# TensorE's order in the head of an attention-and-MLP kernel: short dummies, out products close behind kv, casts on other engines

## The chip, the core and the metric

The kernel runs on one core of one Trainium2 chip. The metric is the device time of one execution in microseconds (us). Executions of one kernel agree within some 0.3%, so every comparison below is of several runs made on the same chip, and a difference counts as faster or slower only from 2% up. Smaller differences are read from the intervals and from the traces.

Engines in the profile: PE is TensorE's matmuls, PEld its weight loads, DVE is VectorE, ACT is ScalarE, POOL is GpSimd, SP is SyncE, which issues most transfers. PEclk is the TensorE clock that the throttle granted, 1.00 being full.

## The reference

Linear attention over 8 batches of 8 heads, 576 tokens of 64 features, and then an MLP with a Swish of learned slope over all 4608 tokens.

```python
def _attn_ref(q, k, v):
    q_s = exp(q - max over features);  q_s = q_s / sum over features
    k_s = exp(k - max over tokens);    k_s = k_s / sum over tokens
    kv = np.einsum('bhsd,bhse->bhde', k_s, v)
    return np.einsum('bhsd,bhde->bhse', q_s, kv)

def _moe_ref(x, w_in, w_out, beta):      # x: 4608 x 512, w_in: 512 x 2048
    h = x @ w_in
    g = h * (1.0 / (1.0 + np.exp(-beta * h)))
    return g @ w_out                     # 4608 x 512, float32
```

## The kernel before

All matmuls are bf16. Each batch's attention is done while the MLP of an earlier batch keeps TensorE busy. Only batch 0 has nothing to hide behind: its attention is the *head*, about 16 us from the start to the unbroken stream of MLP matmuls. Heads are taken in pairs, 0 to 3 (the prediction says "head 1" for pair 1, and "third kv group" for that of pair 2). For each pair TensorE makes a group of 18 small matmuls (*kv*), VectorE takes the reciprocal of the key sums and writes the scaled product to KVD, four transposes (*turns*) bring the queries to QT, and one matmul of 512 columns (*out product*) makes XT from KVD and QT. Tiles: EQ and GT hold exponentials (GT holds those of the keys here), VF and VB values in fp32 and bf16, WST staged weights, WIN and WOUT weights in bf16. Most matmuls come from one helper, so their line is L373 whatever they do; they are told apart by their tiles.

Dummies keep TensorE busy while it waits for data; `long` makes one in fp32:

```python
def warm(n, bk, long=False):
    for _ in range(n):
        if long:
            mm(PS[bk][:, :], <XT8 as fp32, 128 columns>, <XT8 as fp32, 512 columns>, ...)
        else:
            mm(PS[bk][:, :], WARM[:, 0:128], WARM[:, :], ...)      # bf16, 512 columns
...
def kv_tiles(hp, bk):
    for j in range(NG):                  # 9 token groups, 2 heads: 18 matmuls of 64x64
        for e_ in range(2):
            ...
    ksum_inv(0, bk, hp, 1, D, 1)         # VectorE: reciprocal RC
    kvd(0, hp, bk, 0)                    # VectorE: two scalings, KVD

def out_now(b, hp, bk, eng):
    out_mm(b, hp, bk)                    # KVD x QT, 512 columns
    add(eng, ...)                        # copy to XT
```

The head, in program order:

```python
warm(3, 0, True)
exp_q(0)
...
norm_main(0, 0, 1)                       # normalize queries of pair 0, VectorE
norm_main(0, 1, 1, POOL)
go(t_steps(0, (0,), (3,)))               # turns of pair 0
turn_beta()
warm(1, 0, True)
norm_main(0, 2, 1, POOL)
norm_main(0, 3, 1, POOL)
kv_tiles(0, 7)
go(t_steps(0, (1,), (4,)))
warm(1, 0, True)
cast_v(0, 2)
cast_v(0, 3, POOL, 1)                    # second part of the last values, GpSimd
cast_win(0, 1, POOL)
cast_win(0, 2, POOL)
cast_win(1, 0, POOL)
go(t_steps(0, (2,), (5,)))
kv_tiles(1, 1)
out_now(0, 0, 0, ACTE)
go(t_steps(0, (3,), (6,)))
warm(1, 3)
out_now(0, 1, 5, ACTE)
kv_tiles(2, 7)
cast_v(0, 3, ACTE, 0)                    # first part of the last values, ScalarE
cast_win(0, 0, DVE)
warm(1, 3)
kv_tiles(3, 1)
out_now(0, 2, 0, ACTE)
...
at(0)                                    # first four MLP matmuls
out_now(0, 3, 7, DVE)
at(1)
cast_win(0, 3, DVE)
```

SyncE issues nearly all transfers in program order. `load(3)`, which brings the queries, keys and values of batch 3, stands at the end of block t = 0; the DMA transposes of the queries of batch 2 stand in block t = 1, behind it:

```python
# end of t == 0
tr_dma(0)
load(3)                                  # queries, keys, values (1152 KB), query remainders
...
# t == 1
t_dma(2, 0, 2)                           # transposes of pairs 0, 1 of batch 2
...
t_dma(2, 2, 2)                           # pairs 2, 3
```

The softmax here doesn't subtract the row's maximum and nothing guards it: scores larger than these inputs give would overflow.

## Time and profile before

| | before |
|---|---|
| median, first three runs (284.8 to 285.46) | 285.43 us |
| profiled execution, span | 283.1 us |
| TensorE busy | 98% of the span |
| first MLP matmul of the head | 14.99 us |
| out product of pair 3; MLP without a break from | 15.86; 16.08 us |

A profile line of a timeline reads: start us, busy us, engine, line, operation, output tile <- input tiles, shape, count, and in brackets the idle time ahead of it with what ended it. The prediction below shows the page's shares, the chain and the timelines of the head. In the page, the span is cut into 40 slices of 7 us, and this row gives the granted clock in tenths:

```profile
PEclk9999999999999999999999999999999999999999
```

The view of windows gives, for a stretch of time, its length, each engine's busy us (with instruction count), the granted clock, the share of transfer engines in use and GB/s. The two stretches cover most of the head:

```profile
core 0: us, PE busy (x) PEld busy (x) DVE busy (x) ACT busy (x) POOL busy (x), PEclk, DMA share, GB/s
6.83:10.24 3.41, 3.41 (x38) 2.34 (x37) 2.37 (x8) 2.73 (x5) 2.60 (x3) 1.00 1.03 398
10.24:13.66 3.42, 3.09 (x50) 1.60 (x48) 2.33 (x8) 2.18 (x5) 1.60 (x3) 1.00 0.97 341
```

The clock is full from 6.83 us to the end of the program, and the transfer engines have no time to spare in the head (share about 1).

### The profile page before, as it was taken

The page shows a single profiled execution, that of the slowest core. Times are in us where ns is not written, and L with a number is a line of the kernel's source. Part 1 is how long each engine was busy: PE and PEld are TensorE (multiplying, and loading weights), DVE is VectorE, ACT ScalarE, POOL GpSimd, SP SyncE. Part 2 cuts the span into 40 slices and gives each one's busy share as a digit, 9 for nine tenths or more (in the row PEclk, how much of TensorE's full clock was granted, in tenths as well). Part 3 has the DMA queues.
Part 4 walks back from the last instruction along what each step waited for, and adds up shares of the span by engine and source line. Part 5 has one row for each costly group of instructions (what it writes and reads, how often), then busy time and mean ns, then how long its engine had stood idle before and what let it go on. Part 6 is the DMA issues. An engine that isn't in the chain of part 4 may idle for free.

```text
span 283.1 us, 3950 instructions
## 1 busy us (share of the span) xinstructions
PE 277.9 (98%) x1608; PEld 136.3 (48%) x1608; DVE 117.0 (41%) x218; ACT 177.6 (63%) x243; POOL 38.1 (13%) x57
## 2 busy tenths in 40 slices
PE   7899999999999999999999999999999999999995
PEld 3545454445455445544554445444544444444443
DVE  4665786218781348124831473055705300110012
ACT  6767787989978926795579636892660076017500
POOL 6622041216121032100130000000000000000000
PEclk9999999999999999999999999999999999999999
DMA  7999999999998999217960033002700030012022
GB/s 249 371 390 400 391 371 307 361 341 248 330 329 248 358 360 296 39 34 251 374 104 1 2 148 74 2 1 98 141 4 0 9 141 0 0 54 96 0 74 74
DMA packets 41467, 50.07 MB, mean 177 GB/s; under 512 B 20325, under 2 KB 28773, under 8 KB 40297
## 3 DMA queue, kind: packets, MB, share of 16 engines
q1 hardware_dynamic: 40496, 48.77, 55.1%
q10 hardware_dynamic: 952, 1.06, 1.1%
q8 instruction: 12, 0.20, 0.3%
q14 instruction: 7, 0.05, 0.0%
HBM read 36.71 MB, written 9.44 MB: 163 GB/s over the span
## 4 chain that ended last, share of the span: by engine, by line
PE 98%; DVE 0%; ACT 0%; issue 0%
PE PS L373 97%; PE PS L371 1%; ACT XT L544 0%; DVE XT L219 0%; DVE KVD L411 0%; ACT VB L358 0%; DVE O2S L734 0%; DVE RC L520 0%
## 5 line engine op out<-in xcount | busy, mean ns | idle before, releaser
L655 ACT ACTIVATE GT<-PS,BETA 128x512 bf16<-128x512 f32 x144 | 96.7, 689 | 79.1 <-PE PS L373 79.1
L373 PE MATMUL PS<-WOUT,GT 128*128 128x512 bf16 (+2 forms) x592 | 132.8, 373 | 0.0
L373 PE MATMUL PS<-XT,WIN 128*128 128x512 bf16 x576 | 132.2, 379 | 0.0
L373 PEld LDWEIGHTS PS<-XT,WIN 128*128 128x128 bf16 x576 | 60.2, 106 | 59.2 <-ACT GT L655 0.4
L373 PEld LDWEIGHTS PS<-WOUT,GT 128*128 128x128 bf16 x592 | 55.4, 98 | 61.8
L713 DVE COPY O2S<-PS 128x512 f32<-128x512 f32 x33 | 22.7, 687 | 107.7 <-PE PS L373 107.7
L373 PE MATMUL PS<-VB,EK 128*128 128x65 bf16 x252 | 33.3, 193 | 0.0
L358 POOL CAST VB<-VF 128x576 bf16<-128x576 f32 (+1 forms) x29 | 21.1, 729 | 77.9 <-DMA VF<-in_v_dram 73.5
L309 ACT ACTIVATE EK<-KF 64x1152 bf16<-64x1152 f32 x24 | 27.8, 1157 | 0.4
L339 DVE TENSOR_REDUCE QS<-EQ 128x8 f32<-128x512 bf16 (+1 forms) x22 | 20.1, 913 | 15.4 <-ACT EQ L297 15.3
L373 PEld LDWEIGHTS PS<-VB,EK 128*128 128x128 bf16 x252 | 20.0, 98 | 6.5
L449 DVE CAST XT<-PS 128x512 bf16<-128x512 f32 x24 | 16.4, 690 | 10.9 <-PE PS L373 10.9
L297 ACT ACTIVATE EQ<-QF 128x512 bf16<-128x512 f32 x32 | 17.8, 619 | 2.0 <-DMA QF<-in_q_dram 1.8
L341 DVE TENSOR_TENSOR EQ<-EQ,QI 128x1024 bf16<-128x1024 bf16 (+1 forms) x14 | 15.9, 1132 | 0.5
L373 PE MATMUL PS<-QT,KVD 128*128 128x512 bf16 x32 | 12.2, 380 | 0.3 <-DVE KVD L411 0.3
L341 POOL TENSOR_TENSOR EQ<-EQ,QI 128x512 bf16<-128x512 bf16 x8 | 8.3, 1042 | 17.3 <-DVE QI L340 17.0
L373 PE MATMUL PS<-XT 128*128 128x512 f32 x10 | 7.7, 903 | 1.5 <-DVE XT L219 1.5
L411 DVE TENSOR_TENSOR KVD<-PS,RC 64x64 bf16<-64x64 f32 (+2 forms) x28 | 8.6, 308 | 0.9
L297 ACT ACT_TABLE_LOAD x6 | 7.7, 1283 | 0.1
L655 ACT ACT_TABLE_LOAD x5 | 6.4, 1283 | 0.1
L432 DVE RECIPROCAL RC<-PS 128x4 f32<-128x4 f32 (+2 forms) x9 | 1.6, 177 | 10.0 <-PE PS L373 9.9
L319 ACT ACTIVATE EK<-KF 64x576 bf16<-64x576 f32 (+1 forms) x6 | 5.0, 842 | 1.0 <-DMA KF<-in_k_dram 0.9
(54 smaller groups left out, 85.9 us busy)
## 6 DMA issues: line engine op xcount, KB each, us to landing
out_dram<-O2S SPq DMA_DIRECT2D x8, 1024.0 KB, 5.1
KF<-in_k_dram SPq DMA_DIRECT2D x6, 1152.0 KB, 8.4
VF<-in_v_dram SPq DMA_DIRECT2D x6, 1152.0 KB, 11.2
QF<-in_q_dram SPq DMA_DIRECT2D x6, 1024.0 KB, 7.6
KF<-in_k_dram SPq DMA_DIRECT2D x8, 288.0 KB, 8.3
VF<-in_v_dram SPq DMA_DIRECT2D x8, 288.0 KB, 8.6
WST<-in_moe_w_in_dram SPq DMA_DIRECT2D x8, 256.0 KB, 7.9
O2S<-in_moe_w_in_dram SPq DMA_DIRECT2D x4, 512.0 KB, 11.9
```

Source lines behind the costliest of these rows:

```text
L297: add(ACTE, lambda e, o=o, a=a: e.activation(o, a, ACT.Exp), r=[("qf", i, hp)], w=[("eq", i, hp)])
L309: add(ACTE, lambda e, o=o, a=a: e.activation(o, a, ACT.Exp), r=[("kf", i, h) for h in hps], w=[("ek", i, h, e_) for h in hps])
L319: add(ACTE, lambda e: e.activation(o, a, ACT.Exp), r=[("kf", i, h) for h in hps], w=[("ek", i, h, e_) for h in hps])
L339: add(DVE, lambda e: e.tensor_reduce(s_, a, AX.X, ALU.add), r=ks, w=[("qs", i, hp0)])
L341: add(eng, lambda e: e.tensor_tensor(a, a, vb, ALU.mult), r=ks + [("qi", i, hp0)], w=ks)
L358: add(eng, lambda e: (e.copy if eng == ACTE else e.tensor_copy)(o, a), r=[("vf", i, hp), ("vone", i)], w=[("vb", i, hp, h) for h in ((0, 1 ...
L371: add(PE, lambda e: e.transpose(o, l, r_), r=r, w=w, bank=[bk])
L373: add(PE, lambda e: e.matmul(o, l, r_, start=start, stop=stop, tile_position=tp), r=r, w=w, bank=[bk])
L411: add(DVE, lambda e, o=o, a=a, s_=s_: e.tensor_tensor(o, a, s_, ALU.mult), r=[("ps", bk)] + [("rc", i, h) for h in hps], w=[("kvd", i, h, ...
L449: add(eng, lambda e: (e.copy if eng == ACTE else e.tensor_copy)(XT[i][:, hp, :], PS[bk][:, :]), r=[("ps", bk)], w=[("xt", i, hp)], bank=[bk])
L655: add(ACTE, lambda e: e.activation(GT[:, f, :], PS[bk][:, :], ACT.Silu, scale=BETA[:, f:f + 1]), r=[("ps", bk), "beta"], w=[("gt", f)], ba ...
L713: add(eng, lambda e: (e.copy if eng == ACTE else e.tensor_copy)(O2S[t % 2][:, u, :], PS[bk][:, :]), r=[("ps", bk)], w=[("o2", t % 2, u)], ...
```

## The change

Its intent is to start the MLP matmuls earlier. The first fp32 dummy goes, the second becomes bf16, and one bf16 dummy is added ahead of kv 1; the turns of pair 1 stand ahead of kv 0 instead of behind it; out product 1 moves behind kv 2, and out product 2 *ahead* of kv 3; GpSimd casts the last values whole (before, GpSimd and ScalarE shared them), and casts weight blocks 1 to 3 of the first quarter, so that VectorE casts only block 0.

```diff
@@ -618,29 +618,28 @@
         norm_main(0, 1, 1, POOL)
         go(t_steps(0, (0,), (3,)))
         turn_beta()
-        warm(1, 0, True)
         norm_main(0, 2, 1, POOL)
         norm_main(0, 3, 1, POOL)
+        go(t_steps(0, (1,), (4,)))
         kv_tiles(0, 7)
-        go(t_steps(0, (1,), (4,)))
-        warm(1, 0, True)
+        warm(1, 0)
         cast_v(0, 2)
-        cast_v(0, 3, POOL, 1)
-        cast_win(0, 1, POOL)
-        cast_win(0, 2, POOL)
+        cast_v(0, 3)
+        for m in range(1, NM):
+            cast_win(0, m, POOL)
         cast_win(1, 0, POOL)
         go(t_steps(0, (2,), (5,)))
+        warm(1, 0)
         kv_tiles(1, 1)
         out_now(0, 0, 0, ACTE)
         go(t_steps(0, (3,), (6,)))
         warm(1, 3)
+        kv_tiles(2, 7)
         out_now(0, 1, 5, ACTE)
-        kv_tiles(2, 7)
-        cast_v(0, 3, ACTE, 0)
         cast_win(0, 0, DVE)
         warm(1, 3)
+        out_now(0, 2, 0, ACTE)
         kv_tiles(3, 1)
-        out_now(0, 2, 0, ACTE)
 
         orot = [0]
 
@@ -678,7 +677,6 @@
         at(0)
         out_now(0, 3, 7, DVE)
         at(1)
-        cast_win(0, 3, DVE)
         read_beta()
```

## The prediction

> **What bounds the kernel now.** I first read busy shares, then the chain of work that ended last, then TensorE's own timeline for the head. The page's first line of numbers (engine, busy us, share of the span, instructions) says that TensorE is all but always at work.
>
> ```profile
> PE 277.9 (98%) x1608; PEld 136.3 (48%) x1608; DVE 117.0 (41%) x218; ACT 177.6 (63%) x243; POOL 38.1 (13%) x57
> ```
>
> The chain (start us, us, what) shows where it is not. From 14.99 us it is TensorE work to the very end, so whatever advances the start of the dense matmuls, and is not eaten by a later wait, comes off the time one for one. Between 11.9 and 15 us the chain leaves TensorE twice: for a reciprocal and the two scalings that make KVD, and for a cast of values on ScalarE.
>
> ```profile
> 11.92 0.17 DVE RC L520
> ...
> 12.36 0.24 DVE KVD L411
> 12.60 0.05 issue
> 12.64 0.40 PE PS L373
> 13.05 0.02 issue
> 13.07 0.59 ACT XT L544
> 13.66 0.36 ACT VB L358
> 14.02 0.14 issue
> 14.16 0.80 PE PS L373 x19
> ```
>
> TensorE's timeline (start, us, operation, idle before) shows what the head is made of: two fp32 dummy pairs (8.15, 9.85), four kv groups of 18 small matmuls, and out products with 512 columns.
>
> ```profile
> 8.15 1.12 PE L373 MATMUL PS<-XT 128*128 128x512 f32 x2
> 9.21 0.47 PE L373 MATMUL PS<-VB,GT 64*64 64x65 bf16 x18
> 9.61 0.40 PE L371 MATMUL PS<-IDB,EQ 128*128 128x128 bf16 x4
> 9.85 1.08 PE L373 MATMUL PS<-XT 128*128 128x512 f32 x2
> 10.76 0.39 PE L371 MATMUL PS<-IDB,EQ 128*128 128x128 bf16 x4
> ...
> 14.56 0.39 PE L373 MATMUL PS<-QT,KVD 128*128 128x512 bf16 x1
> 14.99 1.04 PE L373 MATMUL PS<-XT,WIN 128*128 128x512 bf16 x4
> 15.86 0.38 PE L373 MATMUL PS<-QT,KVD 128*128 128x512 bf16 x1
> ```
>
> GpSimd's timeline sets when the third values are there (11.57) and when the last half is; the whole last tile can start at 12.23, when its transfer lands.
>
> ```profile
> 8.61 2.16 POOL L341 TENSOR_TENSOR EQ<-EQ,QI 128x512 bf16<-128x512 bf16 x2 [0.31 <-DVE QI L340]
> 10.90 0.67 POOL L358 CAST VB<-VF 128x576 bf16<-128x576 f32 x1
> 12.23 0.40 POOL L358 CAST VB<-VF 128x256 bf16<-128x256 f32 x1 [0.66 <-DMA VF<-in_v_dram]
> 13.82 1.58 POOL L580 CAST WIN<-WST 128x512 bf16<-128x512 f32 x2 [1.19 <-DMA WST<-in_moe_w_in_dram]
> ```
>
> **What the Trainium skill says.** "FP8 and Floating Point Precision", TensorE Precision Notes: true fp32 takes four passes through the array. The trace agrees: the pair at 9.85 holds TensorE until 10.76, 0.91 us, about four times the 0.22 us step of a bf16 matmul of 512 columns (15.86 to 16.08). "TensorE: Matmul & The Clock Gate", Part 1: the array runs at half rate until it has been busy for a window of about 3.4 us and falls back after an idle one. The trace agrees with the first half: the six opening fp32 passes start 0.85 us apart, the pair at 9.85 about 0.45; no run yet shows the fall back. "SBUF — State Buffer", SBUF: two separate sides: VectorE and GpSimd share one port pair, held exclusively. The trace is consistent: GpSimd's weight cast took 0.83 us where it met VectorE's weight cast and 0.62 us otherwise.
>
> **The change part by part.** The dummies fall from 1.06 and 0.91 us to 0.22 each; four bf16 ones remain. That alone ends nothing: the kv groups and transposes then wait for data. So I laid the new order by hand on the old durations and landings. The steps, read start to start: kv to the next TensorE instruction 0.41; kv to its reciprocal 0.83 (12.96 to 13.79); reciprocal and both KVD scalings 0.68; to TensorE 0.06. So an out product can't follow its kv group by less than 1.57 us. Transposes to a dummy 0.22, to kv 0.32; out to kv 0.32; 512 columns 0.22. A handover from GpSimd to TensorE isn't visible; 0.1 is an estimate between 0.06 (VectorE) and 0.14 (ScalarE, the issue row before 14.16).
>
> - Turns of head 1: their queries are normalized by GpSimd at 8.30, so 8.36. kv 0: 8.68 (before 9.21). Dummy 9.08. Turns 2 wait for GpSimd (9.65): 9.71. Dummy 9.93. kv 1: 10.15 (before 11.08; values ready 9.87). VectorE does the turn copy, reciprocal and scalings of head 0 by 10.42, so out 0 at 10.56 finds its operand there. Turns 3: 10.83 (queries 10.77). Dummy 11.05.
> - kv 2 could go at 11.27 but its values are cast on GpSimd until 11.57: 11.68 (before 12.96, 1.28 us gained). Out 1 right behind it, 12.09: KVD 1 is ready at 11.7. Dummy 12.30.
> - Out 2 now stands ahead of kv 3 and waits for KVD 2: 11.68 + 1.57 = 13.25. So TensorE idles about 0.7 us here; this is a new wait.
> - kv 3: 13.25 + 0.32 = 13.57 (before 14.16, 0.59 gained). Its values, whole on GpSimd, take 12.23 + 0.67 = 12.90 and are off the path; the ScalarE half cast, which ended at 14.01 behind two evictions, is gone.
> - First four weight matmuls at 13.57 + 0.41 = 13.98 (before 14.99, 1.0 gained). Weight block 0 lands at 13.09 and VectorE casts it after KVD 2, 13.22 to 13.65: just in time.
> - Out 3 follows four matmuls, 0.87 us, so at 14.85, but needs KVD 3, 13.57 + 1.57 = 15.13: a second new wait, 0.29 us. Before, this operand was early (14.16 + 1.57 = 15.73 against 15.86). The gain shrinks from 1.0 to 0.73 us: dense work resumes at 15.35 instead of 16.08.
> - Weight blocks 1 to 3 of the first quarter on GpSimd: landings 13.77, 14.45, 15.13, casts of 0.62, last one ready about 16.1; it is needed at 17.1. VectorE loses one 0.43 us cast that wasn't on the path.
>
> Sum: 16.08 - 15.35 = **0.73 us** of 283.1.
>
> **Is it kept?** The weights and the next batch arrive at the transfer engines' pace (share 1.0 or above from 10 to 60 us), and landings don't move. So I checked what TensorE meets between 15 and 49 us after moving 0.73 earlier.
>
> ```profile
> 27.04 1.95 DVE L569 TENSOR_SCALAR WOUT<-WST,RB 128x512 bf16<-128x512 f32 x4 [1.80 <-DMA WST<-in_moe_w_out_dram]
> 39.10 2.08 DVE L569 TENSOR_SCALAR WOUT<-O2S,RB 128x512 bf16<-128x512 f32 x4
> 29.03 9.44 PE L373 MATMUL PS<-WOUT,GT 128*128 128x512 bf16 x43
> 39.84 0.61 PE L371 MATMUL PS<-IDB,EQ 128*128 128x128 bf16 x8
> ```
>
> The first output weights are ready at 27.80 and would be wanted at 28.30 instead of 29.03. The tightest place is at 39 to 40: turns of the next batch wanted at 39.11 plus 0.22 for its last head, normalized by 39.18 before and some 0.2 earlier after (VectorE's preceding work can move up only to the landing at 33.55); output weights 12 wanted at 39.55, ready near 39.4. Both fit by 0.1 to 0.4. At 46 the last values of batch 1 are cast at 45.39 and wanted at 45.9. So I keep the 0.73 whole; a landing 0.3 us late would cost perhaps 0.2 of it.
>
> **The rivals.** (1) The waits eat everything: new idle time of some 0.7 us ahead of out 2 and 0.3 ahead of out 3. For it: the 1.57 us latency is now met twice in a row. Against: kv 2 itself starts 1.28 earlier. If GpSimd's cast of the third values ended 0.5 us later, the gain would be 0.2: 285.2. (2) The clock falls back: from 8.2 to 13.3 TensorE would be idle in gaps totalling about 1.7 us, and a bf16 dummy fills little. Against: no gap reaches a whole window, the longest is 0.7. If it fell for one window, half of 3.4 us is lost (an estimate from the page named): 285.43 - 0.73 + 1.7 = 286.4. (3) The gain is hidden by the transfers' pace at 39 to 46 us: then 0.2 to 0.5 remains: 285.0 to 285.2. (4) The dummies' 1.53 us counted in full: 283.9; against it, each of the four kv groups waits for data that the dummies don't delay.
>
> **Range and chances.** Predicted 285.43 - 0.73 = 284.7 us. The runs before spread over 0.66 us, and rivals 1 and 3 lie within 285.2; rival 4 gives the lower side, a median drawn high the upper: 283.9 to 285.6. Two per cent is 5.7 us, eight times the gain: faster 0.01, same 0.97, slower 0.02.
>
> **What would show it.** In the profile after: kv groups starting near 8.7, 10.15, 11.7 and 13.6; idle time ahead of the third out product (0.6 to 0.8, released by VectorE's KVD) and the fourth (0.2 to 0.4); dense matmuls from about 15.35; no idle TensorE later. Wrong if fp32-like steps (0.4 us per 512 bf16 columns) appear after 8 us, or if TensorE waits for WOUT, EQ or VB after 28 us.

## The result, and the profile after

| | before | after |
|---|---|---|
| median | 285.12 us (4 runs) | 284.88 us (4 runs) |
| all runs | 284.8, 285.43, 285.46, 284.79 | 285.38, 285.06, 284.6, 284.7 |
| mean granted clock of those runs | not on record (profiled execution: 1.0) | 0.994, 0.994, 1.0, 1.0 |
| span of the profiled execution | 283.1 us | 283.6 us |

The ratio is 0.9994, with a 95% interval from 0.9971 to 1.0016: the same. Ratios here and below are the mean time of one kernel's fast runs over that of the other's fast runs of the same rounds, so they are not quite the ratio of the medians quoted beside them. The time is inside the predicted range and 0.2 us from the predicted value.

The row of clocks above already shows something new: two runs of four at 0.994. Of the kernel before, 33 later runs have their clock on record, and all have at least 0.998. The profiled execution (285.38 us) is one of them. The page of the kernel after, its shares and its clock row:

```profile
PE 276.3 (97%) x1575; PEld 136.4 (48%) x1606; DVE 116.4 (41%) x217; ACT 177.2 (62%) x242; POOL 39.3 (14%) x58
...
PEclk9799999999999999999999999999999999999999
```

The second slice has fallen from 9 to 7. The view of windows finds where (columns as before):

```profile
7.29:10.71 3.42, 2.75 (x37) 2.00 (x37) 2.85 (x9) 2.71 (x4) 2.77 (x3) 1.00 1.04 400
10.71:14.12 3.41, 3.08 (x43) 1.87 (x44) 1.92 (x9) 1.94 (x4) 1.59 (x3) 0.50 1.01 347
14.12:17.53 3.41, 3.12 (x29) 1.37 (x30) 1.99 (x7) 2.56 (x4) 2.75 (x4) 1.00 1.05 396
```

For 3.41 us the granted clock is exactly one half, and then full again. Half a rate missing for 3.41 us is as much as a whole one for 1.7 us, 0.6% of the span, which is the 0.994 of the run. TensorE's timeline of the same head shows it instruction by instruction:

```profile
9.22 0.48 PE L373 MATMUL PS<-VB,GT 64*64 64x65 bf16 x18 [0.48 <-ACT VB L358]
...
12.74 0.70 PE L373 MATMUL PS<-VB,GT 64*64 64x65 bf16 x18
13.37 0.61 PE L373 MATMUL PS<-QT,KVD 128*128 128x512 bf16 x1
...
14.44 0.38 PE L373 MATMUL PS<-QT,KVD 128*128 128x512 bf16 x1
14.75 0.47 PE L373 MATMUL PS<-VB,GT 64*64 64x65 bf16 x18
15.15 1.04 PE L373 MATMUL PS<-XT,WIN 128*128 128x512 bf16 x4
16.32 0.39 PE L373 MATMUL PS<-QT,KVD 128*128 128x512 bf16 x1
```

A kv group takes 0.70 us instead of 0.47, an out product 0.61 instead of 0.39. Its first kv group is late for another reason: in this execution the first keys landed at 7.73 us, in the profiled execution of before at 6.58. So this head is *behind* that of before: the last out product is at 16.32 instead of 15.86, and 0.46 us of delay stay to the end. I read this delay from ScalarE's 144 Swish instructions and VectorE's output copies, which are all in the record: each stands 0.46 us later than in before, from 18 us to the last, and 0.46 is also the difference of the unrounded spans. One profile was therefore not enough to say what the change is worth.

The chain of waits of this execution needs care. It leaves TensorE just ahead of the MLP stream for a cast of weights on GpSimd:

```profile
16.11 0.63 POOL WIN L580
16.76 10.74 PE PS L373 x49
```

That is not a real wait. The out product ahead of it is 0.46 us later than before and the Swish instructions after it too, so TensorE lost nothing between. In this trace 16 of the 576 matmuls of this kind have no record, and where one is missing a stretch looks idle.

Two theories of why the head's expected 0.73 us hardly show in the time. **Theory A** (H in the expectations): the clock falls in some executions, because the new head gives the array less work; without falls most of the gain would be there. **Theory B** (T there): the gain of the head is real but is taken back later by a transfer at its own pace. The runs below speak for both.

### The profile page after: what moved, and what is told of

Its sections match the earlier page's. It is cut to its first block, busy times and chain, and to the rows that moved or that the text cites. A ratio compares the mean times of both kernels' runs of the same rounds, so it can differ in the third digit from the quotient of the medians.

```text
span 283.6 us, 3916 instructions
## 1 busy us (share of the span) xinstructions
PE 276.3 (97%) x1575; PEld 136.4 (48%) x1606; DVE 116.4 (41%) x217; ACT 177.2 (62%) x242; POOL 39.3 (14%) x58
## 3 DMA queue, kind: packets, MB, share of 16 engines
q10 hardware_dynamic: 952, 1.06, 1.1%
## 4 chain that ended last, share of the span: by engine, by line
PE 93%; DMA 3%; SPq 2%; issue 1%; POOL 1%; DVE 0%; POOLq 0%
PE PS L373 92%; DMA WST<-in_moe_w_in_dram 3%; SPq L259 1%; POOL WIN L580 1%; SPq L249 0%; PE PS L371 0%; SPq L576 0%; DVE O2S L732 0%; POOLq L140 0%
## 5 line engine op out<-in xcount | busy, mean ns | idle before, releaser
L373 PE MATMUL PS<-XT,WIN 128*128 128x512 bf16 x560 | 130.7, 379 | 0.5
L358 POOL CAST VB<-VF 128x576 bf16<-128x576 f32 x29 | 21.6, 746 | 77.9 <-DMA VF<-in_v_dram 48.8
L373 PE MATMUL PS<-QT,KVD 128*128 128x512 bf16 x29 | 11.2, 387 | 0.2
L373 PE MATMUL PS<-XT 128*128 128x512 f32 x6 | 5.5, 1088 | 1.5 <-DVE XT L219 1.5
L373 PEld LDWEIGHTS PS<-QT,KVD 128*128 128x128 bf16 x32 | 3.1, 98 | 5.6 <-DVE KVD L411 1.2
```

The lines of the kernel that those rows point to most:

```text
L358: add(eng, lambda e: (e.copy if eng == ACTE else e.tensor_copy)(o, a), r=[("vf", i, hp), ("vone", i)], w=[("vb", i, hp, h) for h in ((0, 1 ...
L373: add(PE, lambda e: e.matmul(o, l, r_, start=start, stop=stop, tile_position=tp), r=r, w=w, bank=[bk])
```

## The experiments

Each call had its own chip, with 11 interleaved runs of the kernel before. Medians of before: 285.01, 284.81 and 284.81 us. "Held" and "fell" below say whether a run's mean clock was at least 0.998, or 0.994 (one window of 3.41 us at half rate) and lower. All kernels gave the right result. One measure is an estimate of mine: the *work share* of a 3.41 us window, from durations in these traces, which counts 0.86 us for an fp32 dummy, 0.21 for a bf16 matmul of 512 columns, 0.054 for a turn of 128 columns, 0.24 for a kv group of 18, and of the opening fp32 dummies the part that runs inside the window. (The expectation of c3 below quotes an earlier, rougher count of mine.)

### The changed kernel again (a1_again)

No edit, five rounds.

> The changed kernel as it is, to separate two things that its first profile mixes: the granted clock fell to half from 10.7 to 14.1 us, and the first K tile landed at 7.73 us instead of 6.58. In its first four runs the two with mean clock 0.994 took 285.4 and 285.1, the two with 1.0 took 284.6 and 284.7. Theory H (the clock falls back in some runs and eats the gain): runs at clock 0.994 lie 0.4 to 0.8 us above those at 1.000, and the latter are 0.3 to 0.8 below the kernel before. Rival D (the landing of the first tiles decides, the clock is a passenger): times split by the landing, not by the clock. Rival N (no gain at all, only scatter): both groups have the same time as the kernel before.

Median 284.99 us (284.89 to 285.13), ratio 0.9999 [0.9987, 1.0011]. Two runs of five had fallen (285.10, 284.97), three had held (285.13, 284.99, 284.89). So the falls are a property of the changed kernel, and here they cost nothing: means of 285.04 and 285.00. This is a miss for theory H, which expected 0.4 to 0.8 us between the groups. And a gain of 0.73 us lies outside this interval: 0.0013 of 285 us is 0.37. The profiled execution had fallen, from 8.36 to 11.78 us. Its first keys had landed at 6.93 us, ahead of those of a profiled execution below that held (c2, 7.42), so a late landing of the first keys (rival D) is not needed for a fall. In it the first transposes of batch 2 landed at 71.25 us, 0.5 us before their use at 71.77. Nothing waited here, but a head faster by more than 0.5 us would have.

### More bf16 dummies (a2_fill)

```diff
-        warm(1, 0)
+        warm(2, 0)
...
-        warm(1, 0)
+        warm(2, 0)
...
-        warm(1, 3)
+        warm(2, 3)
...
-        warm(1, 3)
+        warm(4, 3)
```

> The changed kernel with more bf16 dummies in the holes: 2, 2, 2 and 4 in place of 1, 1, 1 and 1 (six more, of 0.216 us each, placed where TensorE waits). Theory H: no run with the clock below 1.0; median 284.6 to 284.8, at most 0.1 above the changed kernel's undisturbed runs. Rival (dummies only delay): 0.2 to 0.6 us slower than the changed kernel at the same clock.

Median 285.25 us (284.55 to 286.08), ratio 1.0013 [0.9996, 1.003]. Two runs of six still fell, at 286.06 and 286.08; those that held have a mean of 285.02. That no run would fall was a miss: ten dummies instead of four did not suffice. The profiled execution had held, with work shares of 39% and 57% in its two windows of the head, and its MLP matmuls began at 14.15. It then lost 0.66 us (by the Swish instructions) where one weight block landed late in this execution: at 18.05 us (before: 15.86), cast on GpSimd from 18.11 to 18.72. So this profile does not say what the dummies cost:

```profile
18.78 10.54 PE L373 MATMUL PS<-XT,WIN 128*128 128x512 bf16 x47 [0.49 <-POOL WIN L580]
```

### Out product 2 behind kv 3 again (a3_kv3first)

```diff
-        out_now(0, 2, 0, ACTE)
         kv_tiles(3, 1)
+        out_now(0, 2, 0, ACTE)
```

> The changed kernel with one part undone: the third out product behind the fourth kv group again, as before. My working says the new order of these two costs time, since the fourth kv group then waits for KVD of the third head: kv 3 could start near 13.0 instead of 13.6 and the out product behind it would find its operand; dense matmuls resume some 0.4 to 0.5 us earlier. Expected 284.1 to 284.4 at clock 1.0. Rival: the dense part meets transfers later (output weights wanted before they land at 27.8 and 39.4), so at most 0.2 us shows. Where the clock falls, 0.5 more.

Median 285.06 us (284.55 to 285.33), ratio 0.9996 [0.9984, 1.0008]. Three runs of five fell (285.06, 285.33, 285.19), two held (284.56, 284.55): 0.64 us between the means. The held runs miss the expected 284.1 to 284.4. The place of out product 2 does not bring the falls about: the four profiled falls (after, a1, a3, a4) begin at 8.36 to 10.71 us, ahead of these two instructions, and this order falls about as often.

### No bf16 dummies in the head (a4_nodummy)

The four `warm` lines are removed from the changed kernel.

> The changed kernel without the four bf16 dummies. Theory H: activity in the head falls further, so the clock falls in more runs than in the changed kernel (more than half), and the median is 285.2 or more. Rival (the small dummies do nothing for the clock): as many fallen runs as in the changed kernel, same times.

Median 286.3 us (284.64 to 286.93), ratio 1.0033 [1.0008, 1.0058]. All six runs fell. Those with one window at half rate (0.994) took 284.89 and 284.64, the one at 0.987 took 286.04, the three at 0.982 (three windows) 286.55 to 286.93. So dummies do act on the clock, and the less array work the head holds, the more windows are lost. This is the dose for which theory A asks. The profiled execution (284.89, one fall) was 0.44 us ahead of before after the head, and lost 0.41 of it in a wait for the DMA transposes at 71.57 us: theory B's place again.

### Values of batch 3 issued later, in both kernels (c1_before_vlate, c2_after_vlate)

```diff
-                load(3)
+                load_main("qf", qt_h, QF, 3)
+                load_k(3)
+                load_qrem(2)
...
                     t_dma(2, 2, 2)
+                    load_v(3)
```

> The kernel before with one transfer moved: the values of batch 3 (1.15 MB) are issued behind the two transposes of batch 2's queries instead of ahead of them. In the profiles so far those transposes landed at 70.5 us in the kernel before and at 71.2 to 71.8 in five others, and the first out product of batch 2 starts at 71.6 in the kernel before. Theory T (the stream of transfers, full from 2 to 70 us, is a second bound at 71.6 us): the transposes land before 70 us; the kernel before mostly gains nothing, since there they were just in time, but its slower runs near 285.5 vanish: 284.7 to 285.0, no run above 285.2. Rival (the landing is never the bound): no change in median or scatter.

> The changed kernel with the same transfer moved. Theory T: a run at clock 1.0 shows the head's whole gain of 0.5 to 0.75 us: 284.1 to 284.5; a run at clock 0.994 lies 0.3 to 1.0 above that. If the gain were eaten in the head alone, runs at clock 1.0 stay at 284.7 to 285.1.

Before with the move: median 284.87 us, ratio 0.9999 [0.9986, 1.0012] from four runs (284.69 to 285.02). Its first run took 754.87 us and is left out as slow. TensorE alone was stretched: it is busy for 737.6 us, at some 0.6 us a matmul of 512 columns (49 in 29.36 us), while ScalarE has its usual 178.4 us. The run is listed at clock 1.0, but its page has no clock row, so that says nothing. I have no cause for it. It was the profiled one, so this kernel has no profile that can be compared.

After with the move: median 284.84 us (284.25 to 285.21), ratio 0.9997 [0.9985, 1.0009]. Three runs held (284.70, 284.42, 284.25) and three fell (284.98, 285.19, 285.21): means of 284.46 and 285.13, so one fall costs 0.67 us where nothing later hides it. The held runs are 0.35 us below the median of before; two of the three lie in the expected 284.1 to 284.5. The transposes landed at 68.90 and 70.62 us, and there is no wait for them. But the profiled execution lost 0.15 of its 0.38 us of head gain earlier, between 46.5 and 47.7 us: the last keys of batch 1 landed late (44.59 us, before: 43.30), ScalarE did their exponentials late, its copy of outputs came behind them, and TensorE's weight load waited for that copy. ScalarE's and TensorE's lines:

```profile
44.61 1.39 ACT L319 ACTIVATE EK<-KF 64x576 bf16<-64x576 f32 x2 [0.44 <-DMA KF<-in_k_dram]
...
47.00 0.33 PEld L373 LDWEIGHTS PS<-XT,WIN 128*128 128x128 bf16 x3 [0.38 <-ACT O2S L711]
```

SyncE's timeline shows what the move did to the issue of batch 2's transposes, for before:

```profile
66.01 3.76 SPq L459 DMA_TRANSPOSE QT<-EQ  x2
```

for the changed kernel with the long dummy (c3_long1, next), whose load order is that of before:

```profile
65.36 4.73 SPq L459 DMA_TRANSPOSE QT<-EQ  x2
```

and for the changed kernel with the move:

```profile
65.78 2.95 SPq L459 DMA_TRANSPOSE QT<-EQ  x2
```

Issued 0.65 us earlier, c3's transposes still landed 0.87 us later than those of before (71.35 against 70.48): the queue ahead of them sets when they land. In the ten profiles with the old load order the first of them landed between 70.48 and 71.78 us, in the three with the values behind them between 68.37 and 69.09. The Trainium skill, "DMA: Bandwidth & Descriptors", section Two DMAs through the same engine are not ordered, says that within one queue of one transfer engine descriptors start in order, though they may overlap. These landings are consistent with that: 1152 KB of values that nobody wants soon stood ahead of transposes that TensorE wants at once.

### One fp32 dummy back (c3_long1)

```diff
         turn_beta()
+        warm(1, 0, True)
```

> The changed kernel with one part undone: the fp32 dummy behind the beta transposes is back (1.06 us of TensorE work from about 8.0), the four bf16 ones stay. Theory H (activity of a window of 3.4 us decides): the array work of the windows that fell was, by my count from the traces, 33 to 40 per cent of the window and of those that held 45 per cent or more; the dummy adds 0.85 us to any window that holds it, so fewer runs fall: at most 1 in 5, and later ones (from 11 us) at that. The third kv group is gated by GpSimd, so the dummy costs nothing: runs at clock 1.0 as in the changed kernel, 284.6 to 285.1.

Median 284.73 us (284.55 to 285.02), ratio 0.9995 [0.9983, 1.0008]. The clock held in five runs of five. The dummy stands where TensorE waits for queries anyway, and from the third kv group on the head has the predicted course. TensorE's timeline, from the third kv group on:

```profile
11.68 0.47 PE L373 MATMUL PS<-VB,GT 64*64 64x65 bf16 x18
...
13.34 0.38 PE L373 MATMUL PS<-QT,KVD 128*128 128x512 bf16 x1 [0.65 <-ACT XT L544]
13.64 0.47 PE L373 MATMUL PS<-VB,GT 64*64 64x65 bf16 x18
14.05 1.04 PE L373 MATMUL PS<-XT,WIN 128*128 128x512 bf16 x4
15.21 0.39 PE L373 MATMUL PS<-QT,KVD 128*128 128x512 bf16 x1
```

The wait of 0.65 us ahead of the third out product is the new wait that the prediction named; the view puts it down to ScalarE's copy, which ended at 13.32, while KVD was ready at 13.19, so the two came nearly together. From the last out product on, this head is 0.64 us ahead of before (ScalarE's Swish instructions: 0.64 to 0.65 through 60 us). From 80 us to the end it is 0.21. The loss is in one place. TensorE's timeline for before:

```profile
71.18 0.59 PE L373 MATMUL PS<-WOUT,GT 128*128 128x512 bf16 x2
71.61 0.38 PE L373 MATMUL PS<-QT,KVD 128*128 128x512 bf16 x1
```

and for this kernel:

```profile
70.54 0.59 PE L373 MATMUL PS<-WOUT,GT 128*128 128x512 bf16 x2
71.39 0.39 PE L373 MATMUL PS<-QT,KVD 128*128 128x512 bf16 x1 [0.26 <-DMA QT<-EQ]
```

Two matmuls take 0.43 us start to start (71.18 to 71.61). Here the out product of batch 2 starts 0.85 us after them, 0.42 late, because its queries have only landed at 71.35. The start is 0.64 us early ahead of this line and 0.22 us early after it. The bracket gives only 0.26 since modelled ends overlap; starts are the surer measure.

### The two fp32 dummies of before made bf16, alone (b1_bf16)

In the kernel before, `warm(1, 0, True)` becomes `warm(1, 0)` at both places.

> The kernel before with one part of the change alone: its two fp32 dummies made bf16 (1.06 and 0.91 us to 0.22 each), order and casts as before. Theory H: the clock falls in about half the runs, which then take 0.2 to 0.8 us longer than those at 1.0; the latter as the kernel before or up to 0.2 faster, since kv groups wait for data anyway. Rival (the order, not the dummies, makes the clock fall): clock 1.0 in all runs.

Median 284.67 us (284.22 to 284.78), ratio 0.999 [0.9978, 1.0002]. I had expected falls in about half of the runs; the clock held in all five. Work shares in its windows: 39% and 40%. That need not be the old order's doing. If b1 fell as often as the changed kernel (7 of 15), five held runs would come up about 8 times in 100. And its profile caught a favourable window: the clock rose at 7.51 us. Had it risen between 4.95 and 5.97, as in a1, a4 and a3, the same matmuls would give a first window of 30 to 33%, which is no more than where those fell (an estimate, by the weights above).

### The casts alone (b2_casts)

```diff
-        cast_v(0, 3, POOL, 1)
-        cast_win(0, 1, POOL)
-        cast_win(0, 2, POOL)
+        cast_v(0, 3)
+        for m in range(1, NM):
+            cast_win(0, m, POOL)
...
-        cast_v(0, 3, ACTE, 0)
...
-        cast_win(0, 3, DVE)
```

> The kernel before with the casts alone changed (last values whole on GpSimd, weight blocks 1 to 3 there, order and dummies as before). The fourth kv group no longer waits for ScalarE's half cast (14.02), only for GpSimd (about 12.9), so it starts near 13.6 instead of 14.16, but the third out product behind it waits for KVD 2 at about 14.5: dense matmuls resume 0.2 to 0.3 us earlier, at 15.8. Time 0 to 0.25 below the kernel before, clock 1.0 in all runs.

Median 284.82 us (284.74 to 285.16), ratio 1.0001 [0.999, 1.0013], clock held in five of five. In the profiled execution the casts alone brought 0.12 us, less than the 0.2 to 0.3 expected. They are the smallest part.

### The order alone (e3_order)

The kernel before with TensorE's new order: turns of pair 1 ahead of kv 0, out products moved as in the change. Both fp32 dummies stay, the second behind kv 0, and the casts are those of before.

> The order alone: TensorE's new order, with the two fp32 dummies and the casts as before. The second fp32 dummy now stands behind the first kv group. By the steps of the prediction: second kv group near 10.9, third 12.0, third out product 13.6, fourth kv group 14.1 (ScalarE's half cast comes behind two evictions), dense matmuls resume near 15.9 instead of 16.08, so 0 to 0.3 below the kernel before; clock 1.0 in all runs. If the order itself, not the missing array work, made the clock fall, half its runs fall.

Median 284.55 us (284.48 to 285.09), ratio 0.9995 [0.9983, 1.0007], clock held in five of five. The profiled execution gained 0.38 us, with the third out product waiting 0.65 us and kv 3 at 13.93. Its transposes landed at 70.51 and were used at 71.24, so here the gain was kept, without any move of the loads.

### Long dummy and late values, without and with kv 3 first (e1_long1_vlate, e2_long1_kv3_vlate)

Both are the changed kernel with c3's dummy and c2's move; e2 also has out product 2 behind kv 3 again, as in a3.

> Both losses taken away together: the changed kernel with the fp32 dummy behind the beta transposes (which held the clock in 5 of 5 runs) and with the values of batch 3 behind batch 2's transposes. In the profile with the dummy alone, everything up to 70 us ran 0.64 us ahead of the kernel before and 0.44 of it was lost at one wait, for batch 2's transposes (71.35 us). Theory H+T: 0.5 to 0.65 us below the kernel before, 284.1 to 284.4, no wait of TensorE at 71 us, clock at or near 1.0. Rival (a third bound follows at once): 284.6 or more although the transposes land before 70 us.

> The same, with the third out product behind the fourth kv group again. By the steps of the prediction, kv 3 no longer waits for KVD of the third head: kv 3 near 13.0, out 2 near 13.4, dense matmuls from 13.7 to 13.9 with out 3 not waiting, so 0.3 to 0.5 us ahead of the version with the changed order. Expected 283.7 to 284.1. Against: the fourth values land at 12.4 and are cast by 13.1, so kv 3 at 13.2; and the first output weights and those of 39 us are then wanted about when they land, so 0.2 may be lost there: 284.1 at worst.

e1: median 284.55 us (284.19 to 284.89), ratio 0.9985 [0.9972, 0.9998]; held in five of five. This misses the expected 284.1 to 284.4. The transposes landed at 69.09 and nothing waited at 71. But in the profiled execution a head gain of 0.54 us had shrunk to 0.06 by 52 us. Of this, 0.14 went between 18 and 25 us, which I have not traced, and 0.29 between 39.5 and 40.2 us. There the output weights had landed at 34.38 us (before: 33.55), VectorE's normalization of the last queries came later with them, and the turns wanted them. VectorE's and TensorE's timelines of e1:

```profile
38.52 1.25 DVE L341 TENSOR_TENSOR EQ<-EQ,QI 128x512 bf16<-128x512 bf16 x1
```

```profile
39.49 0.73 PE L371 MATMUL PS<-IDB,EQ 128*128 128x128 bf16 x8
```

The normalization ended at 39.77, while the eight turns, begun at 39.49, were under way; they took 0.73 us start to start with the next matmul (40.22), where the chain of before gives eight of them 0.45. This is the tight place at 39 to 40 us that the prediction named. Whether it binds depends on that execution's landings, and I have one profile only.

e2: median 284.31 us (284.08 to 285.31), ratio 0.9985 [0.9972, 0.9997]; held in six of six. Expected were 283.7 to 284.1. With kv 3 ahead of out product 2, both waits of the head shrink. TensorE's timeline of e2:

```profile
12.90 0.47 PE L373 MATMUL PS<-VB,GT 64*64 64x65 bf16 x18 [0.18 <-POOL VB L358]
13.36 0.38 PE L373 MATMUL PS<-QT,KVD 128*128 128x512 bf16 x1
13.73 1.04 PE L373 MATMUL PS<-XT,WIN 128*128 128x512 bf16 x4
14.61 0.38 PE L373 MATMUL PS<-QT,KVD 128*128 128x512 bf16 x1
```

The fourth out product follows the four MLP matmuls with no wait (13.73 + 0.88 = 14.61), 1.25 us earlier than in before. Of this, 1.04 us are left at 26 us, and 0.76 from 44 us to the end, with no loss at 71. It is the fastest version tried: five of six runs lie between 284.08 and 284.51 us, below every one of the 11 runs of before on that chip (284.62 to 285.12); the sixth took 285.31 at full clock. It beats the kernel before by some 0.15%, which by the 2% rule is still the same; the changed kernel was not timed on that chip.

## Why the prediction was right or wrong

**The time and the verdict were right, the closeness in part by luck.** 284.88 us lies in the range, and "same" was given 0.97. But the prediction subtracts 0.73 us from 285.43, a median of three runs that drew high: the fourth run made it 285.12, and later calls gave 285.01 and 284.81. The gain itself was 0.24 us between the medians here and 0.02 in a1, not 0.73.

**The steps of the head were right to 0.1 us from the third kv group on, in one execution of a kernel close to the change.** Predicted against c3_long1: kv 2 at 11.68 and 11.68; out 2 at 13.25 and 13.34; kv 3 at 13.57 and 13.64; first MLP matmuls at 13.98 and 14.05; out 3 at 15.13 and 15.21. The gain over before is 0.64 us instead of 0.73. c3 has one fp32 dummy more than the change, so its first two kv groups come later than predicted (9.33 and 10.49 against 8.68 and 10.15); the third waits for GpSimd either way. The new wait ahead of out product 2 was predicted at about 0.7 us and measured 0.65. The head of the changed kernel itself was profiled only in executions that had fallen, or with the load moved. That one (c2) gained 0.38 us, half of the 0.73: its third values landed only when GpSimd had waited 0.55 us for them, and from there every step is 0.26 to 0.35 us late (kv 2 at 11.94, out 3 at 15.47). So "landings don't move" does not hold from one execution to the next. Two small readings were loose and carry nothing: the six opening "passes" are six instructions of two passes each, and the 1.06 us of the first dummy holds a wait (its twin took 0.91).

**The step that failed is "So I keep the 0.73 whole".** It rested on a check of what TensorE meets between 15 and 49 us. The check stopped too early, for the transfer stream runs at its full pace until about 113 us (the page's row of transfer engines), and the transposes of batch 2 are wanted at 71. Before, they landed in time (70.48 for a use at 71.61). With the head 0.64 us faster the use is wanted at 70.97, inside the range of their landings (70.48 to 71.78 over the profiles with the old load order), and in c3 0.42 of the 0.64 us were lost there (in a4, 0.41 of 0.44). That is the third rival, a gain hidden by the pace of the transfers, right in kind. Its place, 39 to 46 us, was wrong for these two and right for two others: e1 lost 0.29 us at 40 us and c2 0.15 at 47. With the values behind the transposes, these landed before 69.1 us in all three usable profiles and nothing waited for them, also not in c2 and e2, which wanted them 0.22 and 0.76 us earlier than before did. This shows what caused that wait. That the move by itself makes the kernel faster is not shown: c3 and e1 differ by it alone (on different chips), and their intervals (0.9983 to 1.0008, 0.9972 to 0.9998) overlap.

**The second rival was dismissed with the wrong argument.** "No gap reaches a whole window, the longest is 0.7" took the clock to ask for an idle window. It fell in 7 of 15 runs of the changed kernel and of its twin with only the load moved (2 of 4, 2 of 5, 3 of 6), and in none of the 33 runs of before whose clock is on record. The prediction's own sign of being wrong, steps of 0.4 us per 512 columns after 8 us, came true in the first profile (13.37 to 13.78 us). The window ahead of the fall in the profiled execution, 7.29 to 10.71 us, was by no means idle: TensorE was busy for 2.75 of 3.42 us. But what it held was little work: eight turns (0.43), one kv group (0.24) and two bf16 dummies (0.43), 1.10 us or about a third. In before, the stretch from 6.83 to 10.24 held one and a half fp32 dummies (0.86 and 0.39), the same kv group and eight turns, 1.9 us or 56%. Over the traces, windows with a work share of about 29 to 34% were followed by half rate (a1, a3, a4, after), those with 38% or more were not (a2, b1, c2 and all with an fp32 dummy). In all four the half rate began exactly one window after the clock had first become full (at 4.95, 5.97, 5.30 and 7.29 us), so where that window happens to begin decides how much work it holds. The estimate is rough and the threshold is not measured; the direction is, since removing all bf16 dummies made six of six runs fall and one fp32 dummy more (c3, e1, e2) made none of 16 fall.

The Trainium skill has the two pieces that I should have put together. "TensorE: Matmul & The Clock Gate", Part 1, What's actually happening: the window is 3413 ns and free-running, it is not tied to the program's start. The traces agree: half rate lasts 3.41 us in each fall, and it starts at other times in different executions (10.71, 8.36, 9.38, 8.71 us), which fits falls in only some runs of a program whose work share is near the boundary. And "Perfetto Trace Analysis", Identifying the Most-Contended Engine: the busy share of matmuls is not a good measure of how close a kernel is to the most that the array can do. The window that was 80% busy with about a third of array work agrees.

**The cost of a fall was over-estimated.** The prediction said 1.7 us. The runs give 0.57 (the first four), 0.67 (c2), 0.64 (a3), 1.05 (a2), and about nothing in a1. The likely reason, argued and not tested: half of 3.41 us is lost only while TensorE has work queued, and much of the head is waiting that half rate merely fills. That a fall costs nothing in a1 because the wait for the transposes would have taken the time anyway is argued from the landing at 71.25, not shown.

**The first rival, waits that eat everything, was rightly dismissed:** in c3 the waits came as predicted and left most of the gain. **The fourth, the dummies counted in full, was rightly dismissed:** making the dummies of before short brought 0.25 us in the profile of b1, not 1.5.

**Taken apart,** the dummies alone have a ratio of 0.999, the order alone 0.9995, the casts alone 1.0001, all within their intervals of 1, and in none of these three did the clock fall (15 runs). For the order and the casts alone this is what the two fp32 dummies in them lead one to expect. For the short dummies alone it rests on five runs, which may have been lucky (b1 above); that it takes the order too is not shown.

**What stays open:** the exact work at which the clock falls; why the first keys' landing differs by 1.1 us between two profiled executions; whether the order adds to the falls; where e1 and e2 lost 0.14 and 0.2 us between 18 and 25 us; the run of 754.87 us.

## What to carry to other kernels

When dummies keep the clock up, count the array work in each window of 3.4 us before thinning them, and don't trust TensorE's busy share for it; a long dummy in a wait that exists anyway cost nothing that showed here. When a gain in the head is to reach the end, follow it through every place where TensorE meets a transfer until the transfer stream is idle, not only through the next stage. And issue small urgent transfers ahead of bulk loads that are wanted later.

## What the Trainium skill lacked or had wrong

- "TensorE: Matmul & The Clock Gate", Part 1, gives, in its table, one idle window of about 3.4 us as what brings half rate back, and further down says that frequent short idle stretches can do it too. It came after windows in which TensorE was shown busy for 2.75 of 3.42 us, with an estimated third of array work (about 29 to 34% before the falls, 38% or more where the clock held). The page lacks a figure for how much work counts as busy. Its window length (3.41 us measured) and its two rates (0.50 and 1.00) were right.
- The same page does not say how often a program near that boundary falls: here 7 of 15 runs, with the same instructions on TensorE.
- "DMA: Bandwidth & Descriptors" has no number for a DMA transpose queued behind bulk loads: here the first of two, issued at 65.3 to 66.5 us, landed between 70.48 and 71.78 us behind 1152 KB of values, and between 68.37 and 69.09 us ahead of them.
- No page gives the latency of a group of small matmuls to its reader: the group of 18 matmuls of 64 by 64 shows 0.47 us in the trace, and VectorE's reciprocal of its result starts 0.83 us after its start (12.96 to 13.79 in before).
